# Loading the weights of K and V first: an attention and MLP kernel on one Trainium2 core, with its input DMAs rearranged and one contraction index permuted

## The chip, the cores and the metric

The kernel runs on one core of one Trainium2 chip. The metric is the device time of one execution in microseconds. Before the change it is 720.49 us, the median of three runs (720.48 to 720.58).

The engines are called PE (TensorE, matmul; PEld is its weight load), DVE (VectorE), ACT (ScalarE), POOL (GpSimd) and SP (SyncE, which here only issues DMAs). Each runs its own list of instructions in the order in which they stand, and waits on semaphores for the others. ACT can issue DMAs too; SP and ACT each have a DMA queue of their own.

## The reference

```python
def _A_ref(x, wq, wk, wv, wo):            # x: 1 x 2048 x 512, 32 heads of 16, one K and one V for all heads
    q = (x @ wq).reshape(B, S, H, Dh).transpose(0, 2, 1, 3)
    k = x @ wk
    v = x @ wv
    p = softmax(einsum("bhqd,bkd->bhqk", q, k) * Dh ** -0.5)
    o = einsum("bhqk,bkd->bhqd", p, v)
    return o.transpose(0, 2, 1, 3).reshape(B, S, H * Dh) @ wo

def _B_ref(x, w1, b1, w2, b2):            # w1: 512 x 1792
    return gelu(x @ w1 + b1) @ w2 + b2

xn = layernorm(x)
return x + _A_ref(xn, wq, wk, wv, wo) + _B_ref(xn, w1, b1, w2, b2)
```

All inputs are bf16.

## The kernel before

The kernel has two parts. The first 26 us are a front part that loads the inputs, normalizes x, transposes it, and makes K, V and the first queries. Behind it stands a long loop of scores (PE, line 1086), exponentials (ACT at line 1110, DVE at 1141 with POOL at 1161) and the product with V (PE, line 1154), into which the remaining queries, the MLP and the output projections are woven.

**x and its tiles.** x is 2048 rows of 512 features. It stands in `x_sb` as 16 tiles of 128 rows, a row on a partition. It is loaded in eight pieces, x0 to x7, of two tiles and 256 KB each. The string `X_Q` says for each piece whether SP ("s") or ACT ("a") issues it.

**Layernorm.** For most tiles DVE makes the statistics (`bn_stats`, line 858, then `bn_aggr`, 872); for two tiles ACT does with two passes (855, 865). ACT turns the variance into 1/sigma (877, 879), POOL makes the negated mean `nm` (876, 861) and `nmr` (881). The normalized tile `xn`, which lies in the buffer `ub`, is written by POOL, DVE (both line 895) or ACT (891), as the string `XN_ENG` says.

**Transposes.** PE transposes each tile in four blocks of 128 x 128 (line 914) into PSUM, with the tile as the stationary operand and an identity as the moving one; DVE or ACT (921, 919) copies the result to `xnT`. In `xnT[p, d, s]`, partition p of block d holds one feature of row s. All products that follow contract over this feature: K with `wkp` (line 743, moving 128x512 or 128x256), V and K of single rows with `wvk` (line 743, moving 128x32), the first queries with `wqp` (743), all others with `wq_sb` and the MLP with `w1_sb`. So each of these weights must hold the same feature on the same partition p of the same block d.

**Weights of K and V.** `wvk` holds the 16 columns of wv and of wk for each of the four blocks. POOL copies the wk half into `wkp`, four times side by side (line 810).

**Dummy matmuls.** In the front part the planner also puts matmuls of zeros into PE's order (line 1522, `pro_filler`), where it expects PE to be idle. They are fixed in the order like all others.

**What sets the order.** Every step is recorded with its reads and writes, an estimated duration `occ` and an estimated delay `lat` until others see its result. `Prog.schedule` then plays the program through with these estimates and writes each engine's instructions down in the order that comes out, with the tables (`PRO_DUE` for the front part, `DTAB` and others for the loop) as priorities. On the chip the order is fixed. DMAs are steps of the engine that issues them; `due` and `lat` of a DMA are thus only numbers of this planner.

The places that the prediction speaks of: DVE's first three `bn_stats` wait for x0, x2 and x1, in this order; POOL's line 810 waits for the DMA of wk; PE's dummies at 1522 follow the transposes at 914.

Of the kernel before, what the change touches and what calls it, by code (L numbers as in the profile page):

```python
# [10 lines left out]
P = 128  # L11
# [87 lines left out]
HA = 58  # L99
HB = 168  # L100
LNEXP_SET = 6
X_Q = "sassssss"
X_LAT = (3.1, 3.3, 3.5, 3.6, 3.7, 3.8, 3.8, 3.8)
LAND = (3.8, 4.7, 5.6, 6.4, 7.2, 8.0, 8.7, 9.4)
XN_ENG = "pdpppapadpddddpp"
LN_B = (((0,), "d"), ((1,), "a"), ((2,), "d"), ((3,), "d"), ((4,), "a"), ((5, 8), "d"), ((6,), "d"), ((7,), "d"), ((9,), "d"), ((10,), "d"), ((11,), "d"), ((12,), "d"), ((13,), "d"), ((14,), "d"), ((15,), "d"))
# [23 lines left out]
class Prog:  # L130
# [19 lines left out]
    def add(self, eng, fn, r=(), w=(), acc=None, dma=None, occ=0.1, lat=0.15, allow=1.0, kind=None, tag=None, after=(), due=None, lock=False, docc=0.0, accs=(), chain=None, job=None):  # L150
        op = _Op()
        op.job = job
        op.lock, op.docc = lock, docc
        op.eng, op.fn = eng, fn
        op.stream = dma or eng
        op.amt = 16 if dma else 1
        op.need = bool(dma)
        op.ticket = None
        op.occ, op.lat, op.allow, op.kind, op.tag = occ, lat, allow, kind, tag
        op.idx = len(self.ops)  # L160
        op.done = False
        op.due = due
        op.rel = None
        op.pm = any(k == ("bank", 7) or k[0] == ("bank", 7) for k in (*w, *accs, chain or ("",)))
        deps, sdeps = {}, {}

        def dep(o, raw):
            if o is None or o is op:
                return
            if o.stream == eng == "pe":  # L170
                sdeps.setdefault(id(o), (o, False))
                return
            deps[id(o)] = o
            sdeps[id(o)] = (o, True)

        for k in r:
            dep(self.writer.get(k), True)
            for o in self.accs.get(k, ()):
                dep(o, True)
        for k in w:  # L180
            dep(self.writer.get(k), False)
            for o in self.readers.get(k, ()):
                dep(o, False)
            for o in self.accs.get(k, ()):
                dep(o, False)
        for k in (*((acc,) if acc is not None else ()), *accs, *((chain,) if chain else ())):
            dep(self.writer.get(k), False)
            for o in self.readers.get(k, ()):
                dep(o, False)
        if chain:  # L190
            self.writer[chain] = op
        op.deps = list(deps.values())
        for o in op.deps:
            o.need = True
        for k in w:
            self.writer[k] = op
            self.readers[k] = []
            self.accs[k] = []
        for k in r:
            self.readers.setdefault(k, []).append(op)  # L200
        for k in (*((acc,) if acc is not None else ()), *accs):
            self.accs.setdefault(k, []).append(op)
        for o in after:
            sdeps.setdefault(id(o), (o, kind != "gelu"))
        if self.in_chain:
            o = self.chain.get(eng)
            if o is not None:
                sdeps.setdefault(id(o), (o, False))
            self.chain[eng] = op
        op.sdeps = list(sdeps.values())  # L210
        self.ops.append(op)
        return op
# [401 lines left out]
def bass_parallel_sum__grouped_kv_mqa__dense_activation_gelu__prompt_kernel(  # L614
# [15 lines left out]
    S, D = xf.shape  # L630
    F = B_w1.shape[1]
    assert (S, D, F) == (2048, 512, 1792)
    H, Dh = 32, 16
    NT = S // P
    DT = D // P
# [9 lines left out]
    bf, f32 = dt.bfloat16, dt.float32  # L645
    i16, i32 = dt.int16, dt.int32

    with ExitStack() as es:
        def sb(shape, dtype, name):
            return es.enter_context(nc.sbuf_tensor(name, shape, dtype))  # L650
# [3 lines left out]
        ubs = (ub, x_sb)  # L654
        xn = ub[:, 0:8, :]
        xnT = sb([P, DT, S], bf, "xnT")
        wvk = sb([P, DT, 2 * Dh], bf, "wvk")
        oTp = sb([P, NPR, TBW], bf, "oTp")
        wkp = oTp[:, 1, :].rearrange("p (d a n) -> p d a n", d=DT, a=4)
        wq_sb = sb([P, DT, D], bf, "wq_sb")  # L660
# [5 lines left out]
        w1_sb = sb([P, DT, F], bf, "w1_sb")  # L666
        w2_sb = sb([P, FT, D], bf, "w2_sb")
        b1row = sb([P, P], bf, "b1row")
        b1T = sb([P, FT], f32, "b1T")
        ident = sb([P, P], bf, "ident")  # L670
# [47 lines left out]
        def bank(b, n=1):  # L718
            return pAll[:, b * 512:(b + n) * 512]
# [4 lines left out]
        add = pr.add  # L724

        def B(b):
            return ("bank", b)
# [9 lines left out]
        def mm(o, l, rh, start, stop, r=(), w=(), tp=None, skip=False, occ=0.216, allow=1.5, **ak):  # L737
            kw = {}
            if tp is not None:
                kw["tile_position"] = tp  # L740
            if skip:
                kw["skip_group_check"] = True
            return add("pe", lambda e: e.matmul(o, l, rh, start=start, stop=stop, **kw), r, w, occ=occ, lat=dlat[1],  # L743
                       allow=allow, **ak)
# [26 lines left out]
        def dma(eng, o, i, stream, r=(), w=(), lat=2.2, allow=1.0, **kw):  # L771
            return add(eng, lambda e: e.dma_start(o, i), r, w, dma=stream, occ=0.7, lat=lat, allow=allow, **kw)

        x_view = xf.rearrange("(t p) d -> p t d", p=P)
        for i in range(8):
            e = X_Q[i]
            dma("sp" if e == "s" else "act", x_sb[:, 2 * i:2 * i + 2, :], x_view[:, 2 * i:2 * i + 2, :], f"d_x{i}",
                w=[("x", 2 * i), ("x", 2 * i + 1)], lat=X_LAT[i], due=0.0)
        dma("sp", wvk[:, :, Dh:2 * Dh], A_wk.rearrange("(k p) n -> p k n", p=P), "d_wk", w=["wk_s"], due=0.1, lat=3.0)
        dma("sp", wvk[:, :, 0:Dh], A_wv.rearrange("(k p) n -> p k n", p=P), "d_wv", w=["wv_s"], due=0.2, lat=3.0)  # L780
        dma("sp", wq_sb[:], A_wq.rearrange("(k p) n -> p k n", p=P), "d_wq", w=["wq"], due=0.4, lat=8.0)
        dma("sp", w1_sb[:], B_w1.rearrange("(k p) n -> p k n", p=P), "d_w1", w=["w1"], due=0.5, lat=9.0)
        dma("sp", w2_sb[:], B_w2.rearrange("(k p) n -> p k n", p=P), "d_w2", w=["w2"], due=0.7, lat=15.0)

        def setup(fn, r=(), w=(), occ=0.16, due=0.0, lat=0.1, **kw):
            return add("pool", fn, r, w, occ=occ, lat=lat, due=due, **kw)
# [19 lines left out]
        for g0, g1, f, kw in ((0, Q0_SPLIT, dve, dict(n=Q0_SPLIT * TBW // 2)), (Q0_SPLIT, NGR, setup, dict(occ=0.24 * (NGR - Q0_SPLIT)))):  # L806
            if g0 < g1:
                f(lambda e, g0=g0, g1=g1: e.memset(QT[:, g0:g1, :].rearrange("p g n -> p (g n)").bitcast(f32), 0.0),
                  w=[(k, g, j) for k in ("QT", "QTm") for g in range(g0, g1) for j in range(HG)], **kw)
        setup(lambda e: e.tensor_copy(wkp[:, :, :, 0:Dh], wvk[:, :, Dh:2 * Dh].unsqueeze(2).to_broadcast([P, DT, 4, Dh])),  # L810
              r=["wk_s", "wkp"], w=["wkp"], occ=0.35, due=2.0)

        setup(lambda e: e.tensor_copy(ident_f[:], ident[:]), r=["ident"], w=["ident_f"])
# [20 lines left out]
        def act_set():  # L834
# [4 lines left out]
                    n=1500, due=0.01)  # L839
# [62 lines left out]
        def x_T(ts, bk, eng):  # L902
            n = len(ts)
            for ti in ts:
                normed(ti)
            c = slice(ts[0] * P, (ts[-1] + 1) * P)
            parts = ((0, 2, bk, "a"), (2, 4, (bk + 1) % 3, "d")) if eng == "s" else ((0, DT, bk, eng),)
            for d0, d1, bk, eng in parts:
                m = (d1 - d0) * n
                pT = bank(bk)[:, 0:m * 64].bitcast(bf)  # L910
                for k, ti in enumerate(ts):
                    for d in range(d0, d1):
                        o = ((d - d0) * n + k) * P
                        add("pe", lambda e, ti=ti, d=d, o=o, pT=pT: e.transpose(pT[:, o:o + P], xn[:, ti % 8, d * P:(d + 1) * P], ident[:]),  # L914
                            r=[("u", 0, ti % 8), "ident"], w=[B(bk)], occ=0.069)
                src, dst = pT.rearrange("p (k n) -> p k n", k=d1 - d0), xnT[:, d0:d1, c]
                w = [B(bk)] + [("xnT", ti, h) for ti in ts for h in range(d0 // 2, d1 // 2)]
                if eng == "a":
                    act(lambda e, src=src, dst=dst: e.activation(dst, src, ACT.Copy), w=w, n=m * P)
                else:  # L920
                    dve(lambda e, src=src, dst=dst: e.tensor_copy(dst, src), w=w, n=m * P, mode=2)
# [12 lines left out]
        def vbank(a, b):  # L934
            return (pO[:, a * 32:b * 32], "O") if a < NVA else (bank(5)[:, (a - NVA) * 32:(b - NVA) * 32], B(5))
# [42 lines left out]
        def v_tiles(ts):  # L978
            for ti in ts:
                for d in range(DT):  # L980
                    mm(vbank(ti, ti + 1)[0], xnT[:, d, ti * P:(ti + 1) * P], wvk[:, d, :], d == 0, d == DT - 1,
                       r=["wv_s", "wk_s", ("xnT", ti, d // 2)], w=[vbank(ti, ti + 1)[1]], occ=0.036, kind="v")

        def wq_first():
# [8 lines left out]
        for _, _, kind, a in sorted(steps, key=lambda s: s[:2]):  # L993
# [15 lines left out]
            due=0.0)  # L1009
# [8 lines left out]
        for va, vb_ in ((0, NVA), (NVA, NT)):  # L1018
# [3 lines left out]
                n=(vb_ - va) * Dh, mode=2)  # L1022
# [445 lines left out]
        first, n = None, 0  # L1468
        for t in range(NTILE):
            if is_d[t]:  # L1470
                first, n = (t, 1) if n == 0 else (first, n + 1)
# [41 lines left out]
        for g in range(4):  # L1513
            mm4(pM, oT[:, g * P:(g + 1) * P], wol[:, g, :], False, g == 3, r=[("oTl", g // 2)] + WOL,
                w=[B(7)], due=0.0)
# [48 lines left out]
```

## Time and the profile before

| | |
|---|---|
| median of 3 runs | 720.49 us |
| the profiled execution's own time | 722.47 us |
| its span, first to last instruction | 720.6 us |
| first exponential of the loop (ACT, line 1110) | at 26.25 us |
| PE, DVE, ACT, POOL busy | 98%, 97%, 98%, 63% of the span |
| DMA in the first fortieth of the span (18 us) | 280 GB/s |
| DMA over the whole span | 33 GB/s |

In a timeline or a chain a row begins with the start in us from the span's start and the duration in us; then come engine, line, operation and what it writes and reads. A bracket at the end tells how long the engine was idle before and what ended that. A busy PE is not PE at its peak, since matmuls overlap: the distance between their starts tells the pace.

### The profile page before, as it was taken

What the parts mean: (1) busy time and instruction counts of PE and PEld (TensorE: products, weight loads), DVE (VectorE), ACT (ScalarE), POOL (GpSimd) and SP (SyncE); (2) the same over time, 40 slices, a digit from 0 to 9 for tenths busy, and PEclk for the clock granted to TensorE, in tenths of its full rate; (3) what the DMA queues carried; (4) which work ended last, traced back from release to release, by engine and by line L of the source; (5) the groups of instructions that cost most, each with busy time, mean ns of one, the idle gap of its engine ahead of it and who ended that gap; (6) DMA issues with size and microseconds to landing.
All of it is one profiled execution on the core that took longest, in us unless ns stands there. A gap on an engine that the chain in (4) does not pass through costs nothing.

```text
span 720.6 us, 22619 instructions
## 1 busy us (share of the span) xinstructions
PE 706.1 (98%) x9224; PEld 219.9 (31%) x9224; DVE 699.6 (97%) x1387; ACT 703.9 (98%) x762; POOL 451.0 (63%) x739
## 2 busy tenths in 40 slices
PE   7999999999999999999999999999999999999998
PEld 4332232222243332223222232222233222222233
DVE  7899999999998999999999999999999999999986
ACT  6899999999999999999999999999999999999997
POOL 7455556777633446687777645676775786766531
PEclk9999999999999999999999999999999999999999
DMA  8300100101011010010101110110100110111111
GB/s 280 108 10 17 26 16 10 33 13 29 10 35 30 24 33 18 12 30 19 37 11 26 46 39 19 25 19 16 24 17 17 26 32 18 32 24 33 26 31 40
DMA packets 36254, 23.59 MB, mean 33 GB/s; under 512 B 17768, under 2 KB 32568, under 8 KB 36152
## 3 DMA queue, kind: packets, MB, share of 16 engines
q1 hardware_dynamic: 35880, 21.89, 12.1%
q8 instruction: 74, 1.21, 0.7%
q10 hardware_dynamic: 272, 0.26, 0.1%
q14 instruction: 28, 0.23, 0.1%
HBM read 13.28 MB, written 2.35 MB: 22 GB/s over the span
## 4 chain that ended last, share of the span: by engine, by line
ACT 52%; PE 42%; DVE 3%; POOL 1%; issue 1%; DMA 0%; POOLq 0%
ACT E L1110 49%; PE pAll L1154 21%; PE pAll L1086 13%; PE pAll L767 6%; PE pAll L749 2%; DVE Dt L1141 2%; ACT ub L1343 1%; ACT x_sb L1348 1%; PE pAll L743 1%; DVE Dt L1194 1%; DMA x_sb<-in_A_x_dram 0%; DVE Dt L1162 0%; PE pAll L914 0%; POOL ub L895 0%; ACT x_sb L1343 0%
## 5 line engine op out<-in xcount | busy, mean ns | idle before, releaser
L1110 ACT ACTIVATE E<-pAll 128x1024 bf16<-128x1024 f32 (+2 forms) x676 | 652.2, 1146 | 2.9 <-PE pAll L1086 1.2
L1161 POOL INT64_ADD Dt<-Dt x671 | 429.0, 648 | 246.8 <-DVE Dt L1141 80.1
L1141 DVE TENSOR_SCALAR Dt<-pAll 128x512 int16<-128x512 f32 (+1 forms) x599 | 414.3, 710 | 6.5 <-PE pAll L763 4.4
L1154 PE MATMUL pAll<-Dt,V 128*32 128x512 bf16 x3120 | 417.1, 383 | 0.0
L1154 PE MATMUL pAll<-E,V 128*32 128x512 bf16 x1424 | 284.5, 385 | 0.5 <-DVE Of L1240 0.4
L1086 PE MATMUL pAll<-QT,KT 32*128 32x512 bf16 x2048 | 266.6, 384 | 5.5 <-ACT E L1110 4.2
L1194 DVE TENSOR_SCALAR Dt<-Dt 128x1024 int16<-128x1024 int16 (+7 forms) x291 | 162.0, 567 | 2.2 <-PE pAll L1154 1.9
L1086 PEld LDWEIGHTS pAll<-QT,KT 32*128 32x128 bf16 x2048 | 66.5, 90 | 276.5 <-ACT E L1110 260.8
L1154 PEld LDWEIGHTS pAll<-Dt,V 128*32 128x32 bf16 x3120 | 106.8, 94 | 115.4 <-issue 79.5
L1162 DVE TENSOR_SCALAR Dt<-Dt 128x1024 int16<-128x1024 int16 (+1 forms) x270 | 90.9, 366 | 0.1
L1154 PEld LDWEIGHTS pAll<-E,V 128*32 128x32 bf16 x1424 | 65.7, 94 | 49.1 <-issue 38.5
L767 PE MATMUL pAll<-xnT,w_sb 128*32 128x512 bf16 x520 | 70.5, 382 | 0.0
L767 PE MATMUL pAll<-w_sb,ub 128*32 128x512 bf16 x364 | 49.4, 381 | 0.0
L763 PE MATMUL pAll<-w_sb,x_sb 32*128 32x512 bf16 x116 | 44.6, 384 | 0.1
L767 PE MATMUL pAll<-w_sb,x_sb 128*32 128x512 bf16 x276 | 42.1, 382 | 0.0
L763 PE MATMUL pAll<-xnT,w_sb 32*128 32x512 bf16 x88 | 33.8, 384 | 0.0
L763 PE MATMUL pAll<-w_sb,ub 32*128 32x512 bf16 x84 | 32.3, 384 | 0.0
L767 PE MATMUL pAll<-wop,oTp 128*32 128x512 bf16 x192 | 29.4, 382 | 0.0
L767 PEld LDWEIGHTS pAll<-xnT,w_sb 128*32 128x32 bf16 x520 | 18.3, 95 | 10.9 <-issue 5.2
L763 PE MATMUL pAll<-xnT,wq_sb 32*128 32x512 bf16 x56 | 21.5, 384 | 0.0
L1320 DVE TENSOR_SCALAR ub<-pAll,b1T 128x512 bf16<-128x512 f32 x28 | 20.9, 747 | 0.0
L767 PE MATMUL pAll<-xnT,wq_sb 128*32 128x512 bf16 x200 | 20.7, 383 | 0.2
(135 smaller groups left out, 361.8 us busy)
## 6 DMA issues: line engine op xcount, KB each, us to landing
w_sb<-in_B_w_dram SPq DMA_DIRECT2D x2, 1792.0 KB, 12.4
OfP<-Of SPq DMA_DIRECT2D x96, 32.0 KB, 2.0
rbP<-rden_rows SPq DMA_DIRECT2D x96, 32.0 KB, 1.9
x_sb<-in_A_x_dram SPq DMA_DIRECT2D x16, 128.0 KB, 2.2
QT<-qp SPq DMA_DIRECT2D x124, 16.0 KB, 1.8
out_dram<-x_sb SPq DMA_DIRECT2D x15, 128.0 KB, 1.7
x_sb<-in_A_x_dram SPq DMA_DIRECT2D x7, 256.0 KB, 5.4
OfP<-Of SPq DMA_DIRECT2D x56, 16.0 KB, 1.9
```

The source lines that it names most:

```text
L743: return add("pe", lambda e: e.matmul(o, l, rh, start=start, stop=stop, **kw), r, w, occ=occ, lat=dlat[1], allow=allow, **ak)
L749: add("pe", lambda e, c=c, j=j: e.matmul(o[c, :], l[:, c], rh, start=start, stop=stop, tile_position=(0, 32 * j)), r, [(k, j) for k in w] ...
L763: add("pe", lambda e, b, c=c, j=j: e.matmul(pM, l[c, :], rh[c, :], start=False, stop=b, skip_group_check=True, tile_position=(32 * j, 0)), ...
L767: add("pe", lambda e, b, c=c, j=j: e.matmul(pM[c, :], l[:, c], rh, start=n == 0, stop=b, skip_group_check=True, tile_position=(0, 32 * j)) ...
L1086: ins = e.matmul(o, l, rh, start=True, stop=True, tile_position=(q0, 0))
L1110: o = act(lambda e: e.activation(E[:, s0:s0 + na, :], bank(b0, na).rearrange("p (a n) -> p a n", a=na), ACT.Exp, scale=LN2 / 128.0), w=[B( ...
L1141: op = dve(lambda e: e.tensor_scalar(Dt[:, s:s + n, :], bank(bk, n).rearrange("p (a n) -> p a n", a=n), float(127 * 128) + SPL_D, SPL_MIN, ...
L1154: add("pe", lambda e, a, b: e.matmul(pO[32 * j:32 * j + 32, :], V1[:, v, kt, :], rhs, start=a, stop=b, tile_position=(0, 32 * j)), r=r + [ ...
L1161: return e.int64_add(d.bitcast(dt.uint64), x.bitcast(dt.uint64), k * 0x0001000100010001 % 2 ** 64)
L1162: return e.tensor_scalar(d, x, float(k), None, ALU.add)
L1194: dve(lambda e, d=view(o, nb), q=view(i, nb), k=k: e.tensor_scalar(d, q, float(k), None, ALU.add), r=keys(i), w=keys(o), n=nb * n * TBW, m ...
L1320: dve(lambda e: e.tensor_scalar(ubs[tb % 2][:, ft, :], pM, b1T[:, ft:ft + 1], None, ALU.add), r=["b1T"], w=M4 + [ukey(tb, ft)], n=TBW + 57 ...
```

## The change

It has three parts.

1. The two DMAs of wk and wv move from SP's queue, behind the seven pieces of x there, to the front of ACT's queue. The piece x1, which ACT issued, becomes the second of eight on SP's queue.
2. The weights wk, wv, wq and w1 are loaded with `(p k) n` in place of `(k p) n`: partition p holds the features 4p, 4p+1, 4p+2 and 4p+3 in its four blocks, in place of p, 128+p, 256+p and 384+p. So a partition reads one unbroken stretch: 128 bytes of wk or wv in place of four of 32, 4 KB of wq in place of four of 1 KB, 14 KB of w1 in place of four of 3.5 KB. `wvk` becomes `[P, 2, DT, Dh]`, with wv and wk in halves of their own.
3. So that `xnT` holds the same features, the transposes take every fourth feature of a row (`d:D:DT`) in place of 128 neighbours. `w2` and `wo` contract over something else and stay.

The planner's `due` and `lat` of the DMAs are set so that its order of everything else comes out as it was; PE's, DVE's and POOL's instructions stand in the same order.

```diff
-X_Q = "sassssss"
-X_LAT = (3.1, 3.3, 3.5, 3.6, 3.7, 3.8, 3.8, 3.8)
+X_Q = "ssssssss"
+X_LAT = (3.1, 3.9, 2.8, 2.9, 3.0, 3.1, 3.1, 3.1)
...
-        wvk = sb([P, DT, 2 * Dh], bf, "wvk")
+        wvk = sb([P, 2, DT, Dh], bf, "wvk")
...
-        dma("sp", wvk[:, :, Dh:2 * Dh], A_wk.rearrange("(k p) n -> p k n", p=P), "d_wk", w=["wk_s"], due=0.1, lat=3.0)
-        dma("sp", wvk[:, :, 0:Dh], A_wv.rearrange("(k p) n -> p k n", p=P), "d_wv", w=["wv_s"], due=0.2, lat=3.0)
-        dma("sp", wq_sb[:], A_wq.rearrange("(k p) n -> p k n", p=P), "d_wq", w=["wq"], due=0.4, lat=8.0)
-        dma("sp", w1_sb[:], B_w1.rearrange("(k p) n -> p k n", p=P), "d_w1", w=["w1"], due=0.5, lat=9.0)
+        dma("act", wvk[:, 1], A_wk.rearrange("(p k) n -> p k n", k=DT), "d_wk", w=["wk_s"], due=-0.1, lat=6.6)
+        dma("act", wvk[:, 0], A_wv.rearrange("(p k) n -> p k n", k=DT), "d_wv", w=["wv_s"], due=0.0, lat=6.6)
+        dma("sp", wq_sb[:], A_wq.rearrange("(p k) n -> p k n", k=DT), "d_wq", w=["wq"], due=0.4, lat=8.7)
+        dma("sp", w1_sb[:], B_w1.rearrange("(p k) n -> p k n", k=DT), "d_w1", w=["w1"], due=0.5, lat=9.7)
...
-        setup(lambda e: e.tensor_copy(wkp[:, :, :, 0:Dh], wvk[:, :, Dh:2 * Dh].unsqueeze(2).to_broadcast([P, DT, 4, Dh])),
+        setup(lambda e: e.tensor_copy(wkp[:, :, :, 0:Dh], wvk[:, 1].unsqueeze(2).to_broadcast([P, DT, 4, Dh])),
...
-                        add("pe", lambda e, ti=ti, d=d, o=o, pT=pT: e.transpose(pT[:, o:o + P], xn[:, ti % 8, d * P:(d + 1) * P], ident[:]),
+                        add("pe", lambda e, ti=ti, d=d, o=o, pT=pT: e.transpose(pT[:, o:o + P], xn[:, ti % 8, d:D:DT], ident[:]),
...
-                    mm(vbank(ti, ti + 1)[0], xnT[:, d, ti * P:(ti + 1) * P], wvk[:, d, :], d == 0, d == DT - 1,
+                    mm(vbank(ti, ti + 1)[0], xnT[:, d, ti * P:(ti + 1) * P], wvk[:, :, d, :], d == 0, d == DT - 1,
```

ACT's order at its beginning, with - before and + now (`wvk` is the tile of the weights of V and K; the last two rows are the first steps of layernorm on ACT):

```order
 L611 UNCONDITIONAL_BRANCH
 L838 ACT_TABLE_LOAD
-L772 DMA x_sb<-in_A_x_dram 128x2x512
+L772 DMA wvk<-in_A_wk_dram 128x64
+L772 DMA wvk<-in_A_wv_dram 128x64
 L855 ACTIVATE oTp,sm<-x_sb 128x512
 L877 ACTIVATE lnv<-mv,epsc 128x1
```

ACT now issues wk and wv where it issued x1, ahead of its first arithmetic.

SP's order at its beginning (`w_sb` stands for w1 and then w2):

```order
 L611 UNCONDITIONAL_BRANCH
-L772 DMA x_sb<-in_A_x_dram 128x2x512 x7
-L772 DMA wvk<-in_A_wk_dram 128x4x16
-L772 DMA wvk<-in_A_wv_dram 128x4x16
-L772 DMA wq_sb<-in_A_wq_dram 128x4x512
-L772 DMA w_sb<-in_B_w_dram 128x4x1792
+L772 DMA x_sb<-in_A_x_dram 128x2x512 x8
+L772 DMA wq_sb<-in_A_wq_dram 128x2048
+L772 DMA w_sb<-in_B_w_dram 128x7168
 L772 DMA w_sb<-in_B_w_dram 128x14x512
 L772 DMA wop<-in_A_wo_dram 128x4x512
```

SP issues one more piece of x and no longer wk and wv; wq and w1 follow one DMA earlier.

More of the change, by code (lines that the diff above doesn't have):

```diff
@@ L778, in bass_parallel_sum__grouped_kv_mqa__dense_activation_gelu__prompt_kernel @@
                 w=[("x", 2 * i), ("x", 2 * i + 1)], lat=X_LAT[i], due=0.0)
-        dma("sp", wvk[:, :, Dh:2 * Dh], A_wk.rearrange("(k p) n -> p k n", p=P), "d_wk", w=["wk_s"], due=0.1, lat=3.0)
-        dma("sp", wvk[:, :, 0:Dh], A_wv.rearrange("(k p) n -> p k n", p=P), "d_wv", w=["wv_s"], due=0.2, lat=3.0)
-        dma("sp", wq_sb[:], A_wq.rearrange("(k p) n -> p k n", p=P), "d_wq", w=["wq"], due=0.4, lat=8.0)
-        dma("sp", w1_sb[:], B_w1.rearrange("(k p) n -> p k n", p=P), "d_w1", w=["w1"], due=0.5, lat=9.0)
-        dma("sp", w2_sb[:], B_w2.rearrange("(k p) n -> p k n", p=P), "d_w2", w=["w2"], due=0.7, lat=15.0)
+        dma("act", wvk[:, 1], A_wk.rearrange("(p k) n -> p k n", k=DT), "d_wk", w=["wk_s"], due=-0.1, lat=6.6)
+        dma("act", wvk[:, 0], A_wv.rearrange("(p k) n -> p k n", k=DT), "d_wv", w=["wv_s"], due=0.0, lat=6.6)
+        dma("sp", wq_sb[:], A_wq.rearrange("(p k) n -> p k n", k=DT), "d_wq", w=["wq"], due=0.4, lat=8.7)
+        dma("sp", w1_sb[:], B_w1.rearrange("(p k) n -> p k n", k=DT), "d_w1", w=["w1"], due=0.5, lat=9.7)
+        dma("sp", w2_sb[:], B_w2.rearrange("(k p) n -> p k n", p=P), "d_w2", w=["w2"], due=0.7, lat=15.7)
         def setup(fn, r=(), w=(), occ=0.16, due=0.0, lat=0.1, **kw):
```

## The prediction

> **What bounds the kernel now.** I read the page first.
>
> ```profile
> span 720.6 us, 22619 instructions
> PE 706.1 (98%) x9224; PEld 219.9 (31%) x9224; DVE 699.6 (97%) x1387; ACT 703.9 (98%) x762; POOL 451.0 (63%) x739
> ```
>
> Three engines are busy for 97 to 98% of the span. The exp loop, which starts at 26 us, has next to no slack, and the change touches none of its instructions. What can move is the moment at which the loop starts. So I read the chain of work for the first 40 us (start, us, what).
>
> ```profile
> 0.80 3.51 DMA x_sb<-in_A_x_dram
> ...
> 9.33 1.38 issue
> ...
> 10.73 0.40 POOL oTp L810
> ...
> 11.60 0.77 POOL ub L895
> 12.41 0.61 PE pAll L914 x4
> ...
> 26.25 7.44 ACT E L1110 x8
> ```
>
> The chain runs through POOL, whose instructions stand in a fixed order. From 9.33 to 10.71 POOL does nothing. The view of waits for this stretch names the cause, and the DMA issues of single stretches tell when each piece lands (after the size: us from issue to landing). The rows are x1 (the ACT one), then on SP's queue x2, x7, wk and wv. The timeline has their issues; the seven x issues on SP take 0.47 of 3.53 us each and follow every 0.51 us from 0.80.
>
> ```profile
> POOL oTp L810 <- DMA wvk<-in_A_wk_dram: 1.4, 1, 1.4
> x_sb<-in_A_x_dram ACTq DMA_DIRECT2D x1, 256.0 KB, 3.8
> x_sb<-in_A_x_dram SPq DMA_DIRECT2D x1, 256.0 KB, 4.0
> x_sb<-in_A_x_dram SPq DMA_DIRECT2D x1, 256.0 KB, 6.6
> wvk<-in_A_wk_dram SPq DMA_DIRECT2D x1, 16.0 KB, 6.3
> wvk<-in_A_wv_dram SPq DMA_DIRECT2D x1, 16.0 KB, 6.0
> 0.80 3.53 SPq L772 DMA_DIRECT2D x_sb<-in_A_x_dram  x7
> 4.37 0.47 SPq L772 DMA_DIRECT2D wvk<-in_A_wk_dram  x1
> 4.88 0.54 SPq L772 DMA_DIRECT2D wvk<-in_A_wv_dram  x1
> ```
>
> So wk lands at 4.37 + 6.3 = 10.7 us, because it stands behind x7, which lands at 3.87 + 6.6 = 10.5. POOL reaches its copy L810 at 9.33 and waits until then. Behind L810 on POOL stand the rows of `nm`, `nmr` and the normalization L895, and PE waits for that.
>
> **The change part by part.**
>
> *The wait on wk goes.* wk is issued first on ACT's queue, at about 0.82. On that queue 256 KB took 3.8 us, so 16 KB is there by 4.6, far ahead of 9.33. POOL gains 1.38 us, and its L895 that ended at 12.37 ends at 10.99. What is late next? The timeline of PE and DVE:
>
> ```profile
> 5.38 1.29 DVE L858 BATCH_NORM_STATS2 stats<-x_sb 128x6 f32<-128x512 bf16 x2
> 8.57 0.70 DVE L895 TENSOR_SCALAR ub<-x_sb,nm,rstd 128x512 bf16<-128x512 bf16 x1
> 9.32 1.03 PE L914 MATMUL pAll<-ident,ub 128*128 128x128 bf16 x8 [0.29 <-DVE ub L895]
> 10.15 1.49 PE L1522 MATMUL pAll<-zeros 128*128 128x256 bf16 x6
> 12.41 0.61 PE L914 MATMUL pAll<-ident,ub 128*128 128x128 bf16 x4 [0.78 <-POOL ub L895]
> ```
>
> PE has transposes (L914) and six dummy matmuls (L1522) ahead of the transposes that wait for POOL. The dummies end at 10.15 + 1.49 = 11.64, and they are in PE's order whether needed or not. So of POOL's 1.38 us only PE's idle time of 0.78, from 11.64 to 12.41, can be gained: **-0.77 us**. PE's own chain is late next: the dummies follow L914 at 9.32, that follows DVE's L895 at 8.57, and that DVE has worked without a break since 5.38, when its second `bn_stats` had waited for x2 (1.31 + 4.0 = 5.3).
>
> *The pieces of x.* Whatever delays x2 takes as much from the gain. Before, x2 was on SP behind x0 while x1 came on the other queue; now x0 and x1 stand ahead of it on one queue, so the same bytes are ahead, plus wk and wv. Price of wk and wv: on SP they landed about 0.2 us each after their predecessor (10.5, 10.7, 10.9) with 512 pieces of 32 bytes; with 128 of 128 bytes I take a quarter to the whole, 0.1 to 0.4 for both. Price of one queue instead of two, from the windows (last column GB/s):
>
> ```profile
> 4.00:4.50 0.50, 0.50 (x4) 0.32 (x3) 0.17 (x1) 0.17 (x1) 0.49 (x3) 1.00 1.09 383
> 4.50:5.00 0.50, 0.50 (x4) 0.15 (x1) 0.50 (x1) 0.50 (x2) 0.40 (x3) 1.00 1.08 342
> 6.00:7.00 1.00, 0.00 (x0) 0.00 (x0) 1.00 (x4) 1.00 (x5) 0.84 (x7) 1.00 1.06 350
> ```
>
> Two queues moved 383 and one 342 to 350: over the 1.5 us in which x1 and x2 arrive that is at most 0.15. x0 alone at the front may land up to 0.3 sooner, which frees nothing, since x2 sets DVE's start. I take **+0.2** (0 to +0.5). x1 itself may come 0.5 later than its 0.82 + 3.8 = 4.6; DVE reads it in the second of the two `bn_stats` of the 5.38 row, at about 6.0, so that is free.
>
> *PE's pace.* The groups of PE from 9 to 16.6 us, then from 16.9 to 25 (mean ns of one behind the bar):
>
> ```profile
> L914 PE MATMUL pAll<-ident,ub 128*128 128x128 bf16 x22 | 3.1, 310 | 1.1 <-POOL ub L895 0.8 <-DVE ub L895 0.3
> L914 PE MATMUL pAll<-ident,ub 128*128 128x128 bf16 x37 | 3.9, 220 | 0.1
> 16.77 0.35 PEld L743 LDWEIGHTS pAll<-wvk,xnT 128*128 128x128 bf16 x10
> 18.38 0.17 PEld L914 LDWEIGHTS pAll<-ident,ub 128*128 128x128 bf16 x3 [0.22 <-ACT ub L891]
> ```
>
> The same transpose takes 310 ns early and 220 late; eight from 9.32 step by 0.104, so PE runs at half pace until about 16.7. If that moment stays, the 0.57 us of work that moves ahead of it costs up to 0.28 more, and PE's idle 0.22 before 18.38 takes part of that: 0.06 to 0.28, I take **+0.15**.
>
> *The transposes read every fourth element.* The stationary operand of all 64 is now strided. A contiguous load of 128 columns steps by (0.35 - 0.10) / 9 = 0.028 us (L743, above), a transpose by 0.104 slow and about 0.055 fast. The load hides behind the matmul ahead of it until it is two to four times as long. I take 0; the other end is a rival below. [...]
>
> *Edits at nothing.* V's matmuls read 2 runs of 16 instead of 32, as many elements. The copy L810 reads the same 64 elements a partition. wq and w1 go in fewer, larger packets and are issued about 0.5 sooner; their readers are far off.
>
> ```profile
> L985 POOL COPY oTp<-wq_sb x1: 396/396/396, 16.8 to 16.8; 128x256 bf16<-128x256 bf16 x1
> wq_sb<-in_A_wq_dram SPq DMA_DIRECT2D x1, 512.0 KB, 6.5
> w_sb<-in_B_w_dram SPq DMA_DIRECT2D x2, 1792.0 KB, 12.4
> L767 PEld LDWEIGHTS pAll<-xnT,w_sb x520: 92/95/97, 41.9 to 533.8; 128*32 128x32 bf16 x174
> ```
>
> wq, issued at 5.46, lands at 12.0 and is read at 16.8; w1 is read first at 41.9.
>
> Sum: -0.77 + 0.2 + 0.15 = **-0.42 us** at the start of the loop. Everything behind 26.25 stands in a fixed order on engines that are full, so the end moves by as much: a span of 720.2 for 720.6. The profiled execution's own time was 722.47, 1.98 above the median of 720.49 (its recording is in it); I take the difference over to the median: 720.07, so 720.1. A measurement of this kernel can tell about 0.2%, 1.44 us, from no change.
>
> **The rivals.**
>
> *PE reaches its full pace earlier (faster).* PE was unbroken for 3.81 us at the front (the 17 dummies, row below) and stayed slow; it was unbroken from 12.41 and was fast 4.3 us later.
>
> ```profile
> 1.33 3.81 PE L1522 MATMUL pAll<-zeros 128*128 128x256 bf16 x17 [1.33 <-POOL mask L825]
> 15.16 1.06 PE L743 MATMUL pAll<-xnT,oTp 128*128 128x512 bf16 x2
> ```
>
> With the idle 0.78 gone, PE works unbroken from about 9.5, so 4.3 us of it are reached at 13.8. Then the work that would stand from 13.8 to 16.2, 2.4 us, could take half, 1.2 less; copies on ACT and DVE between it (about 1 us each) do not shrink, so I take 0.75 of it and drop the term for the pace: -0.57 - 0.75 = -1.3, 719.2 (718.6 to 719.7). [...] 28%.
>
> *Strided weight loads show (slower).* Place: L914. It decides from the point where a load takes longer than the transpose it hides behind, 0.055 to 0.104 us. Four times 0.028 is 0.11: nothing in the slow part, +0.055 for each of the 37 transposes of the later group, +2.0. Eight times is 0.22: +0.12 x 22 + 0.17 x 37 = +8.9 at most. I take the lower: -0.4 + 2.0 = 722.1 and up (721.5 to 729). Nothing in the trace reads a strided stationary operand. 13%.
>
> *The x pieces come later than I take it.* If x2 slips by 0.8 or more, PE's chain is as late as POOL was and the gain is gone: 720.5, and for a slip of 1.0 with x4 and x6, which DVE also meets just landed, 720.8 (720.5 to 721.2). For it: DVE has nothing else to do at 5.38. Against: the same bytes, and wk and wv are 32 KB beside 768. 10%.
>
> *The wait does not go* (wk lands after 9.33 even so): it would need 8.5 us for 16 KB at the front of a queue that gave 256 KB in 3.8. Below 1%, and left out.
>
> **How the numbers follow.** The forecast has 49%, its own range 719.6 to 720.5. Faster by over 0.2% means below 719.05: half of the early-pace case, 0.14. Slower by over 0.2% means above 721.93: nearly all of the strided case and a little of the late x, 0.13. The rest is 0.73. The range from 718.8 to 721.2 holds the forecast, the late x and nearly all of the early pace; it leaves out the strided case and the early pace's lower end, together under 2 in 10.
>
> **What would show it.** Right: no idle time before L810; L810 at about 9.3 to 9.5 on POOL; PE's row L914 x4 at 11.8 to 12.0 with no idle time ahead of it; DVE's second L858 at 5.4 to 5.8; the first E row at 25.7 to 26.0. The early pace would show as 128x512 matmuls of L743 (1.06 us for two at 15.16 before) at the fast duration before 16 us. Strided loads would show as L914 steps above 0.055 late or longer PEld rows. I am wrong if the loop starts where I say and the end moves otherwise, or if x2 lands before 5.3.

## The result and the profile after

The changed kernel is 721.56 us in the median (720.97 to 722.44, 20 runs), before 720.56 (720.14 to 721.86, 20 runs): ratio 1.0014 [1.0007, 1.002]. It is slower by 1.0 us; it was forecast 0.4 us faster. Two later comparisons on other chips gave 1.0005 [0.9996, 1.0014] and 1.0008 [0.9999, 1.0016], medians 0.65 and 0.30 above before. So the loss is 0.3 to 1.0 us by the medians, within the 0.2% that count as no change; only the first of the three intervals excludes 1.

The first profiled execution of the changed kernel took 722.15 us. Its page begins:

```profile
span 720.3 us, 22619 instructions
PE 704.5 (98%) x9224; PEld 219.5 (30%) x9224; DVE 698.8 (97%) x1387; ACT 704.0 (98%) x762; POOL 451.5 (63%) x739
```

The instruction count is that of before, and span and busy times nearly so. The first 26 us look different. POOL's timeline there:

```profile
9.25 0.21 POOL L876 TENSOR_SCALAR nm<-mv 128x1 f32<-128x1 f32 x1 [1.70 <-DVE mv L872]
...
10.78 0.39 POOL L810 COPY oTp<-wvk 128x256 bf16<-128x256 bf16 x1
11.14 0.22 POOL L876 TENSOR_SCALAR nm<-mv 128x2 f32<-128x2 f32 x1
```

L810 no longer waits for wk, yet it starts at 10.78, where it had stood at 10.73 before. POOL's wait has moved upstream: 1.70 us at 9.25, for DVE's `mv`. DVE and PE show why:

```profile
7.14 1.29 DVE L858 BATCH_NORM_STATS2 stats<-x_sb 128x6 f32<-128x512 bf16 x2 [2.45 <-DMA x_sb<-in_A_x_dram]
...
10.82 1.04 PE L914 MATMUL pAll<-ident,ub 128*128 128x128 bf16 x8 [2.58 <-DVE ub L895]
11.66 1.49 PE L1522 MATMUL pAll<-zeros 128*128 128x256 bf16 x6
12.94 0.63 PE L914 MATMUL pAll<-ident,ub 128*128 128x128 bf16 x4
```

DVE's second `bn_stats` waited 2.45 us for x2 and began at 7.14 instead of 5.38. The chain of work to the loop now runs through exactly these rows (start, us, what):

```profile
1.81 5.30 DMA x_sb<-in_A_x_dram
7.14 1.29 DVE stats L858 x2
...
10.82 1.04 PE pAll L914 x8
11.87 1.28 PE pAll L1522 x6
13.15 0.43 PE pAll L914 x4
...
25.97 7.44 ACT E L1110 x8
```

x2 was issued at 1.81 and took 5.30 us. The loop begins at 25.97; its distance to the end of the span is 694.3 us, as in before (720.6 - 26.25 = 694.35). In all but one of the profiles of this study this distance is 694.3 to 694.4 (the exception is in the last section). So all that the change does is done by the first E row.

Seen alone, these two profiles seem to bear the forecast out: the loop begins at 25.97 instead of 26.25, and the span is 720.3 instead of 720.6. That is luck. The profiled execution of before lay 1.98 us above its kernel's median, that of the changed kernel 0.59.

### The profile page after: what moved, and what is told of

It is laid out like the page before. It is cut to its first block, busy times and chain, and to the rows that moved or that the text cites. A ratio compares the mean times of both kernels' runs of the same rounds, so it can differ in the third digit from the quotient of the medians.

```text
span 720.3 us, 22619 instructions
## 1 busy us (share of the span) xinstructions
PE 704.5 (98%) x9224; PEld 219.5 (30%) x9224; DVE 698.8 (97%) x1387; ACT 704.0 (98%) x762; POOL 451.5 (63%) x739
## 4 chain that ended last, share of the span: by engine, by line
ACT 52%; PE 43%; DVE 4%; DMA 1%; issue 0%; SPq 0%
ACT E L1110 49%; PE pAll L1154 21%; PE pAll L1086 13%; PE pAll L767 6%; PE pAll L749 2%; DVE Dt L1141 2%; ACT ub L1343 1%; DMA x_sb<-in_A_x_dram 1%; ACT x_sb L1348 1%; PE pAll L914 1%; DVE Dt L1194 1%; PE pAll L743 0%; DVE Dt L1162 0%; DVE stats L858 0%; ACT x_sb L1343 0%
## 5 line engine op out<-in xcount | busy, mean ns | idle before, releaser
L1194 DVE TENSOR_SCALAR Dt<-Dt 128x1024 int16<-128x1024 int16 (+7 forms) x291 | 160.2, 560 | 2.2 <-PE pAll L1154 1.9
L1162 DVE TENSOR_SCALAR Dt<-Dt 128x1024 int16<-128x1024 int16 (+1 forms) x270 | 89.4, 357 | 0.1
```

What stands on the lines that cost most here:

```text
L1162: return e.tensor_scalar(d, x, float(k), None, ALU.add)
L1194: dve(lambda e, d=view(o, nb), q=view(i, nb), k=k: e.tensor_scalar(d, q, float(k), None, ALU.add), r=keys(i), w=keys(o), n=nb * n * TBW, m ...
```

## The experiments

The theory after the result was D: with x1 moved from ACT's queue to SP's, x2 lands later, and DVE, then PE, wait for it. Its rivals were that the loads of wk and wv beside x are to blame, that the strided transposes cost, or that only the executions or the chips differ; each expectation says which theory it speaks of. Each comparison with before is within one chip. In the table "x2 row" is the start of DVE's second L858 in the profiled execution and "loop" the first E row. The ratio is worked out from the same runs, but it is not the quotient of the two medians: the last two columns can differ by up to 0.4 us. Where an edit moves a DMA, the planner's `lat` numbers move with it, so that the order of everything else stays; the diffs below leave these lines out.

| kernel | x2 row | loop | span | median minus before | ratio |
|---|---|---|---|---|---|
| before2 | 5.54 | 24.31 | 718.7 | one run | |
| rows_only | 5.79 | 25.57 | 719.9 | -0.10 | 0.9994 [0.9985, 1.0003] |
| x_one_queue | 6.38 | 25.32 | 719.7 | +1.41 | 1.0014 [1.0005, 1.0022] |
| x_one_queue2 | 6.54 | 25.98 | 720.3 | +1.22 | 1.0015 [1.0007, 1.0024] |
| x1_on_act | 4.55, x1 7.95 | 26.80 | 721.2 | +1.62 | 1.0019 [1.001, 1.0029] |
| after2 | 6.07 | 24.73 | 719.1 | one run | |
| after3 | 5.55 | 24.85 | 720.5 | +0.65 | 1.0005 [0.9996, 1.0014] |
| after4 | 5.93 | 24.59 | 718.9 | +0.30 | 1.0008 [0.9999, 1.0016] |
| after_old_rows | 5.92 | 25.38 | 719.7 | +0.04 | 1.0001 [0.9992, 1.001] |
| after_old_rows2 | 5.83 | 25.10 | 719.5 | +0.55 | 1.0004 [0.9995, 1.0013] |
| kv_behind_x1 | 5.74 | 25.15 | 719.5 | -0.13 | 0.9997 [0.9988, 1.0005] |
| kv_behind_x1b | 5.74 | 24.57 | 718.9 | -0.17 | 0.9993 [0.9985, 1.0002] |
| x1x3_on_act | 5.73 | 24.38 | 718.7 | -0.23 | 0.9998 [0.9989, 1.0007] |
| x2_behind_x3 | 6.14 | 25.37 | 719.7 | +0.43 | 1.0003 [0.9994, 1.0012] |
| x2_on_act | 5.50 | 24.10 | 718.5 | -0.64 | 0.9993 [0.9984, 1.0002] |
| after_no6 | 5.85 | 25.42 | 719.7 | +1.45 | 1.0019 [1.001, 1.0029] |

**before2** is before once more.

> The kernel before once more, for a second profile of it. The changed kernel's profile has x2 landing at 7.12 us where before had 5.35. Theory A (x2's lateness belongs to the change): here x2 lands at 5.2 to 5.6 us again and wk at 10.5 to 11. Theory B (landings differ that much from execution to execution of one kernel): x2 lands somewhere between 5.3 and 7.2. The moment at which PE's pace rises (16.7 us before, 15.3 after) is expected to differ here by up to some us under both.

It took 720.50 us; the other runs of before on this chip have a median of 720.91. x2 came as theory A has it (row at 5.54), wk earlier than it has it (10.0). The rows on POOL and PE:

```profile
10.04 0.40 POOL L810 COPY oTp<-wvk 128x256 bf16<-128x256 bf16 x1 [0.60 <-DMA wvk<-in_A_wk_dram]
...
10.26 1.38 PE L1522 MATMUL pAll<-zeros 128*128 128x256 bf16 x6
11.72 0.40 PE L914 MATMUL pAll<-ident,ub 128*128 128x128 bf16 x4
```

The wait for wk is 0.60 here instead of 1.38, and PE's four transposes follow the dummies, which end at 11.64, after 0.08 us. wk's DMA row shows where the 0.7 us went (last column: us from issue to landing). It was issued at 4.37 in both, and in the first profile it had taken 6.3:

```profile
wvk<-in_A_wk_dram SPq DMA_DIRECT2D x1, 16.0 KB, 5.6
```

So in this execution the wait that the change removes was hidden behind PE's dummies nearly whole. The first profile, at 722.47, was an execution on the long side. Two kernels below with wk at its old place behind x7, rows_only and x2_behind_x3, agree with the second: POOL goes on to L810 without a wait (at 9.67 and 9.78).

**rows_only** is before with `(p k) n` and the strided transposes, queues as before.

```diff
-A_wk.rearrange("(k p) n -> p k n", p=P)           # wk, wv, wq, w1
+A_wk.rearrange("(p k) n -> p k n", k=DT)
-e.transpose(pT[:, o:o + P], xn[:, ti % 8, d * P:(d + 1) * P], ident[:])
+e.transpose(pT[:, o:o + P], xn[:, ti % 8, d:D:DT], ident[:])
```

> The kernel before with nothing changed but the layout: wk, wv, wq, w1 in whole rows, feature 4p+k on partition p, transposes of every fourth feature; queues as before. Theories Q and S: x2 at 5.3 to 5.6 us, wk some 0.3 us sooner than 10.7, time 0 to 0.4 us below before. Theory R: 0.8 us or more above before, with steps of the transposes over 0.055 us where PE is fast.

-0.10 us, an interval that holds 1. Seven strided transposes at full pace, and seven contiguous ones of before2:

```profile
16.34 0.56 PE L914 MATMUL pAll<-ident,ub 128*128 128x128 bf16 x7
```

```profile
15.04 0.55 PE L914 MATMUL pAll<-ident,ub 128*128 128x128 bf16 x7
```

The strided stationary operand costs nothing that shows. x2's row, at 5.79, is a little later than the 5.3 to 5.6 of Q and S.

**x_one_queue** is before with x1 on SP's queue, behind x0; wk, wv and the later weights keep their places behind the last x, one issue later.

```diff
-X_Q = "sassssss"
+X_Q = "ssssssss"
```

> The kernel before with nothing changed but x1, which is second of eight pieces on SP's queue; wk and wv behind x7 on SP with their old rows. Theory Q: x2 lands at 6.5 to 7.2 us and the time is 0.6 to 1.2 us above before. Theory S: x2 lands at 5.3 to 5.7 us and the time is within 0.3 us of before.

+1.41 us, and the interval excludes 1: this one move gives the loss, a little above theory Q's 1.2. DVE waits for x2:

```profile
6.38 1.29 DVE L858 BATCH_NORM_STATS2 stats<-x_sb 128x6 f32<-128x512 bf16 x2 [1.80 <-DMA x_sb<-in_A_x_dram]
```

But x2 is not what comes last here. wk too is issued 0.5 us later, and the chain of this profile runs through it (start, us, what):

```profile
4.88 5.91 DMA wvk<-in_A_wk_dram
...
10.84 0.10 POOL oTp L810
...
11.70 0.77 POOL ub L895
...
12.52 0.62 PE pAll L914 x4
```

On the way of x2, PE's eight transposes begin at 10.06 (first row), in before2 at 9.43 (second row):

```profile
10.06 1.04 PE L914 MATMUL pAll<-ident,ub 128*128 128x128 bf16 x8 [1.31 <-DVE ub L895]
```

```profile
9.43 1.04 PE L914 MATMUL pAll<-ident,ub 128*128 128x128 bf16 x8 [0.34 <-DVE ub L895]
```

That is 0.63 us later; the four at the chain's end begin 0.80 us later (12.52 against 11.72). So x2 accounts for most of the shift in this profile and wk for the rest. In the changed kernel wk is early, and only the first part is left.

The windows show that the transfers thin out just when x0 and x1 have arrived (last columns: DMA share, GB/s). First before2, then x_one_queue on the same chip, then the changed kernel's first profile:

```profile
4.00:4.50 0.50, 0.50 (x4) 0.33 (x3) 0.06 (x1) 0.06 (x1) 0.49 (x3) 1.00 1.09 385
4.50:5.00 0.50, 0.43 (x4) 0.13 (x1) 0.50 (x1) 0.50 (x2) 0.40 (x3) 1.00 1.08 379
```

```profile
4.00:4.50 0.50, 0.50 (x4) 0.33 (x3) 0.47 (x2) 0.39 (x2) 0.49 (x3) 1.00 0.96 262
4.50:5.00 0.50, 0.50 (x4) 0.15 (x1) 0.08 (x1) 0.07 (x1) 0.50 (x4) 1.00 0.91 227
```

```profile
4.00:4.50 0.50, 0.50 (x4) 0.32 (x3) 0.48 (x1) 0.50 (x2) 0.49 (x3) 1.00 1.12 236
4.50:5.00 0.50, 0.50 (x4) 0.15 (x1) 0.18 (x1) 0.07 (x2) 0.50 (x4) 1.00 0.90 229
```

In before2, with a big piece at the head of both queues, 379 to 385 GB/s run on; in the other two, with one queue of big pieces, it falls to 227 to 262. In the later profiles of the changed kernel (after2, after3, after4) these windows have 254 to 338, so the dip is not always as deep. In the six rows above the DMA share stays at 0.90 to 1.12, so by this measure the DMA engines are not idle meanwhile. What the one queue lacks at that moment the trace does not show.

**x1_on_act** is the changed kernel with x1 back on ACT's queue, but behind wk and wv.

```diff
-X_Q = "ssssssss"
+X_Q = "sassssss"          # order on ACT: wk, wv, x1
```

> The changed kernel with x1 back on ACT's queue, behind wk and wv; whole rows and everything else as changed. Theory Q (x1 on SP's queue ahead of x2 is what makes x2 late): x2 lands at 5.3 to 5.6 us, POOL does not wait for wk, time 0.3 to 0.8 us below before, 720.56 -> about 720.0. Theory S (the small packets of wk and wv at the front are what make x2 late): x2 lands at 6.5 to 7.2 us, time 0.5 to 1.2 us above before. Theory R (the strided transposes cost it): 0.8 us or more above before with x2 at 5.3 to 5.6.

+1.62 us, so this does not cure the loss. x2 came early, but x1 took 6.1 us from its issue, and DVE waited for that one:

```profile
4.55 0.69 DVE L858 BATCH_NORM_STATS2 stats<-x_sb 128x6 f32<-128x512 bf16 x1
7.95 0.69 DVE L858 BATCH_NORM_STATS2 stats<-x_sb 128x6 f32<-128x512 bf16 x1 [2.70 <-DMA x_sb<-in_A_x_dram]
```

Again the third big piece is the late one, whichever it is. None of the three theories had this. To have two queues isn't enough: with wk and wv at the head of ACT's the loss is there too.

**after2**, **after_old_rows**, **kv_behind_x1** and **x1x3_on_act** shared a chip. after_old_rows has the changed queues with the old layout. In kv_behind_x1 x1 stays at the head of ACT's queue and wk and wv, in whole rows, follow it there; x1x3_on_act has x1, x3, wk, wv there.

```diff
-X_Q = "ssssssss"          # order on ACT: wk, wv
+X_Q = "sassssss"          # kv_behind_x1, order on ACT: x1, wk, wv
```

> The changed kernel once more, for a second profile. [...] Theory L (the 7.12 of the first profile was one execution's luck): x2 at 5.4 to 6.0.

> The changed kernel with the old rows: wk and wv first on ACT's queue as 512 pieces of 32 bytes each, all of x on SP's queue, transposes of neighbouring features. [...] Theory R (strided transposes are the cost): time back at or below before.

> Pieces of x as before (x1 first on ACT's queue), wk and wv in whole rows behind x1 on ACT's queue. Theory D: x2 lands at 5.3 to 5.8 us as before, wk by 5.5 us, POOL does not wait for it, and the time is 0.4 to 0.9 us below before. Theory S (small packets of wk and wv among the first transfers stall the engines wherever they stand): x2 at 6 us or later and no gain.

> x1 and x3 on ACT's queue, wk and wv behind them there, the other six pieces on SP's. Theory D: with two queues feeding the engines there is no dip of the DMA rate between 3.75 and 6 us; x2 at 5.0 to 5.6, x4 to x7 by 0.3 us sooner than before; wk by 6.5; time 0.4 to 1.0 us below before. Theory S: the dip is there again, x2 at 6 or later.

The two with x1 at the head of ACT's queue have x2's row at 5.74 and 5.73 and no loss; the two with x1 on SP's queue have it at 6.07 and 5.92. The 6.07 is just past theory L's 5.4 to 6.0 and 1.07 us before the first profile's 7.14; the gains of 0.4 us and more that theory D gave kv_behind_x1 and x1x3_on_act did not come (-0.13 and -0.23). The loss itself hardly showed on this chip (after_old_rows +0.04). That leaves open whether it hangs on the chip, which is rival C of the next expectations.

**after3**, **x_one_queue2** and **after_old_rows2**, on a third chip, repeat the comparison.

> The changed kernel once more, timed on the same chip as the two kernels beside it. Theory D (moving x1 onto SP's queue makes the third piece x2 land 0.5 to 1.8 us later, DVE's statistics wait for it, and PE's whole chain behind them shifts): x2 after 6.0 us, the second DVE L858 after it, PE L914 x4 at 11.9 to 13.0, and the median 0.6 to 1.2 us above before. Rival C (the loss of the first result came from the chip or the executions drawn): within 0.3 us of before.

> Before, with only x1 moved from ScalarE's queue to second place on SP's. Theory D: as the changed kernel, 0.7 to 1.4 us above before, x2 at 6.0 us or later. Rival R (the whole-row loads of wk and wv on the other queue take the place of x's packets and so delay x2): no loss here, since wk and wv stand behind x; x2 at 5.3 to 5.8 us.

> The changed kernel with the old layout of the four weights (wk, wv, wq, w1 in 32-element or 512-element rows, contiguous transposes), queues as changed. Theory D: the queue of x1 alone matters, so it lies within 0.3 us of the changed kernel beside it, and above before by 0.3 us or more. Rival W (the layout of the weight loads matters): it lies near before, as its single earlier comparison had it, while the changed kernel beside it is 0.6 us or more above it.

x_one_queue lost as much as before (+1.22), the changed kernel 0.65 and its old-layout twin 0.55. So the layout makes no difference that shows (against W), and having wk early seems to give back 0.6 of what x1's move costs (721.26 against 721.83). D's lower bound of 0.6 for the changed kernel held by a hair, and the interval holds 1. D's rows were missed in after3's profile: x2's is at 5.55 and the four transposes at 11.41, both sooner than it had them. There the chain runs through x6, a later piece of the one queue. In x_one_queue2 it runs through x3:

```profile
3.86 5.74 DMA x_sb<-in_A_x_dram
...
9.62 1.29 DVE stats L858 x2
```

```profile
2.32 5.88 DMA x_sb<-in_A_x_dram
...
8.21 0.69 DVE stats L858
```

So it is not always x2 that comes last. In after, after2 and after4 it is.

**after_no6** is the changed kernel without the six dummies between L914 x8 and x4.

```diff
-list(self.fill_deps), self.pro_filler, (None, 0)
+list(self.fill_deps), None if 20 <= nfill < 26 else self.pro_filler, (None, 0)
```

> The changed kernel without the six dummy matmuls that stand between the transposes x8 and x4 on PE. By the chain of the changed kernel these six take 1.28 us between the end of the transposes that the late x2 releases and the four that POOL's chain releases, whose input is long there. Theory L (what is late is the chain, and PE's pace is not set by those six): the four transposes start at once behind the eight, the loop starts up to 1.3 us earlier, and the median falls by 0.5 to 1.3 us below the changed kernel. Rival P (the dummies buy PE's full pace): the pace rises one period of 3.4 us later in most executions, and the median is the same as the changed kernel's or up to 0.8 us above it.

722.06 against after3's 721.26: slower by 0.8. The four transposes did not start at once; POOL's chain was late next:

```profile
9.54 1.04 PE L914 MATMUL pAll<-ident,ub 128*128 128x128 bf16 x8 [1.29 <-DVE ub L895]
11.52 0.62 PE L914 MATMUL pAll<-ident,ub 128*128 128x128 bf16 x4 [0.94 <-POOL ub L895]
```

PE idles there for 0.94 us. The windows of this execution and then of after4 (PEclk is the third number from the end) show 26 matmuls at 0.50 where after4 does 37 at 0.85:

```profile
11.50:14.50 3.00, 2.75 (x26) 2.44 (x28) 3.00 (x9) 2.85 (x10) 2.93 (x10) 0.50 0.97 407
```

```profile
11.50:14.50 3.00, 2.72 (x37) 2.24 (x35) 3.00 (x10) 2.70 (x9) 2.84 (x11) 0.85 0.91 382
```

The six dummies are worth more than they cost; the median speaks for rival P. The later rise is seen in one profile of each, so that it is the cause is possible and not shown.

**after4** and **kv_behind_x1b** share a chip with **x2_behind_x3**, which is before with x3 issued ahead of x2 on SP's queue, so that x2 is late for another reason.

```diff
-    w=[("x", 2 * i), ("x", 2 * i + 1)], lat=X_LAT[i], due=0.0)
+    w=[("x", 2 * i), ("x", 2 * i + 1)], lat=X_LAT[i], due=(-0.8, -0.7, -0.5, -0.6, -0.4, -0.3, -0.2, -0.1)[i])
```

> The changed kernel again, beside a kernel that differs from it in x1's queue alone. Theory D: 0.5 to 1.2 us above before; x2 after 5.5 us and later than in the kernel beside it. Rival C (the loss hangs on the chip): within 0.3 us of before here.

> The changed kernel's whole rows and its wk and wv on ScalarE's queue, but x1 stays at the front of that queue as before. Theory D: the loss is x1's move alone, so this one lies 0.5 to 1.3 us below the changed kernel and 0 to 0.3 us below before; x2 at 5.3 to 5.8 us, L810 without a wait. Rival W (any wk and wv beside x at the front cost x its bandwidth): it lies with the changed kernel.

> Before with x3 issued ahead of x2 on SP's queue, x1 on ScalarE's queue as before: x2 lands one step later (6.0 to 6.6 us), with both queues busy at the front, nothing else moved. Theory D (x2's landing itself sets the chain, however it comes late): 0.5 to 1.2 us above before, like x_one_queue, with PE L914 x8 at 9.9 to 10.6. Rival Q (one queue at the front costs in another way than through x2, or the chain has room for a later x2): within 0.3 us of before.

The changed kernel was at 721.21, kv_behind_x1b at 720.74 (-0.47; its highest run, 721.04, is below 7 of the 11 of after4). In both wk is early; what differs is x1's queue, and with it whether wk and wv head ACT's. Their two profiles do not show the loss: x2's rows differ by 0.19 us and the loops begin at 24.59 and 24.57. x2_behind_x3 was 0.43 above before, with nothing moved but x2 and x3, which changed places:

```profile
6.14 1.29 DVE L858 BATCH_NORM_STATS2 stats<-x_sb 128x6 f32<-128x512 bf16 x2 [0.92 <-DMA x_sb<-in_A_x_dram]
...
9.82 1.03 PE L914 MATMUL pAll<-ident,ub 128*128 128x128 bf16 x8 [1.35 <-DVE ub L895]
```

That is D's direction, but under D's lower bound of 0.5, as after4's 0.30 is under its own, and the interval holds 1. By itself it would be weak; it agrees with the rest. Rival C is not excluded as to the size: with x1 on SP's queue and wk early the loss was 1.0, about 0, 0.6 and 0.3 us in the four comparisons.

**x2_on_act** is kv_behind_x1b with x1 and x2 exchanged: x2 at the head of ACT's queue, x1 second on SP's, as the change has it.

```diff
-X_Q = "sassssss"
+X_Q = "ssasssss"          # order on ACT: x2, wk, wv
```

> As kv_behind_x1b, but x2 and not x1 stands at the front of ScalarE's queue, and x1 is second on SP's. Both queues still begin with a big piece. Theory D (x2's landing sets DVE's second L858 and the chain; a big piece at the front of each queue keeps the front full): x2 at 4.3 to 4.8 us, x1 at 5.3 to 5.8, DVE goes on without a wait behind the first tile at about 5.2, PE L914 x8 at 8.8 to 9.1, and the median 0.1 to 0.6 us below before, at or below kv_behind_x1b. Rival S (x1 second on SP's queue is what hurts, whatever stands on ScalarE's): x1 after 6.0 us, DVE waits for it, and the median is 0.4 us or more above before.

720.68 against 721.32 of before on that chip, ratio 0.9993 [0.9984, 1.0002]. DVE no longer waits behind the first tile, though x0 itself came late in this profile, at 4.65:

```profile
4.67 0.70 DVE L858 BATCH_NORM_STATS2 stats<-x_sb 128x6 f32<-128x512 bf16 x1 [1.86 <-DMA x_sb<-in_A_x_dram]
...
5.50 1.25 DVE L858 BATCH_NORM_STATS2 stats<-x_sb 128x6 f32<-128x512 bf16 x2
```

x2 landed at 5.0 and x1 at 6.0, and PE's next transposes began at 9.22, all a little later than expected. So x1's place as second on SP does no harm while a big piece heads the other queue (against S). With kv_behind_x1 and x1x3_on_act this is the best of the versions; all four comparisons came out 0.1 to 0.6 us below before, and none of the intervals excludes that there is no gain. All four lie below the changed kernel's 0.3 to 1.0 above before.

## Why the prediction was wrong

*The term of -0.77, the wait on wk.* The wait went, as said. But the term was at least 0.5 us too big, since it was sized from one execution in which the last pieces of x landed late. In before2 the wait is 0.60 and all of it but 0.08 lies behind the six dummies: kv_behind_x1b, where wk is early and x2 at 5.74, has PE's four transposes at 11.47, before2 at 11.72 (shown above).

```profile
11.47 0.39 PE L914 MATMUL pAll<-ident,ub 128*128 128x128 bf16 x4
```

There is 0.25 us to be had at most, and the medians show 0.1 to 0.2, not clear of nothing. The working put the 1.98 us between that execution and the median down to its recording; before2, also profiled, took 720.50, so it was the execution.

*The term of +0.2 for x2, bound 0.5.* This is the step that failed. The working said "the same bytes are ahead" and priced one queue by steady windows at 0.15. x2's row came 0.2 to 1.8 us later than 5.38 (5.55, 5.93, 6.07, 7.14 in four profiles), over the bound in three of four, and 0.84 later in x_one_queue than in before2. The steady windows (342 to 350 GB/s) do not hold for the first pieces: the rate fell to 227 to 262 when the second piece was in. x2's issue moved from 1.31 to 1.81, by 0.5 us. In the two profiles with only x1 moved its row is later than before2's by more than that, 0.84 and 1.00; the changed kernel's four, 0.01 to 1.60 after it, lie on both sides. So whether one queue costs x2 more than the shift of its issue is not settled by the runs.

*The sum.* With at most -0.25 for wk and 0.2 to 1.8 for x2 in place of -0.77 and +0.2, and the +0.15 for PE's pace as it stood, the sum is a loss of 0.1 us or more.

*The rival of the late x* was the right one. It stood at 10% and gave 720.5 for a slip of 0.8, as a gain of 0.77 given back, and 720.8 for 1.0; its range ended at 721.2, under the 721.56 measured. The slip was 0.2 to 1.8, and there was next to no gain to set against it. The prediction's own "what is late next" named the chain that the changed kernel then showed: x2, L858, L895, L914 x8, the dummies, L914 x4.

*PE's pace.* Neither the fixed moment of 16.7 nor the rival of 4.3 us unbroken work holds. The moment is one thing in one execution and another in the next of the same kernel. kv_behind_x1b and kv_behind_x1 have x2's row at 5.74 both; in the windows they differ:

```profile
11.50:14.50 3.00, 2.70 (x39) 1.93 (x39) 3.00 (x10) 3.00 (x11) 2.92 (x12) 1.00 0.94 387
```

```profile
11.50:14.50 3.00, 3.00 (x29) 2.49 (x28) 2.86 (x9) 2.70 (x8) 2.84 (x11) 0.50 0.95 388
```

The first has 39 matmuls at full pace from 11.5 to 14.5, the second 29 at half, and their loops begin at 24.57 and 25.15. The other profiles sort the same way. Where PEclk stays at 0.50 for 3.41 us after its fall, the loop begins at 24.10 to 24.85 (seven profiles); where it stays for 6.83 us, at 25.10 to 25.98 (eight). Three profiles (before, x_one_queue, x1_on_act) can't be sorted so: PEclk is 1.00 throughout the front, though their eight transposes at 9 to 11 us take 1.03 to 1.05 us, against 0.62 and 0.64 for eight behind the rise in before2 and kv_behind_x1b.

This goes a good way to explain how 0.4 us of a late x2 can become up to 1 us in the median: work that comes later may more often be caught by the second stretch at half pace. The profiles with two stretches have a mean granted clock of 0.995, those with one 0.997 or 0.998 (after3, with its second fall, apart). 25 of 42 executions of the changed kernel had 0.995 or less, 46 of 130 of before, and 10 of 56 of the five kernels with a big piece at the head of both queues and whole rows. In before those executions have a median of 721.51, the others 720.63. The others include executions at 0.999 or 1.000, which by the three profiles above need not have run faster, so the counts are rough. That the late x2 causes the shift in these shares is an inference from the counts; no run set the phase of the pace. Nor does a run separate the late x2 from the gap that it leaves: with x1 behind it x0 lands sooner (first L858 at 3.69 to 3.79 in the changed kernel, 4.33 and 4.45 in before), so PE stands idle for 1.05 to 2.58 us ahead of its eight transposes, in before for 0.29 and 0.34.

*The strided loads* cost nothing that shows (rows_only: -0.10 us, seven transposes in 0.56 us against 0.55; the 0 was the author's estimate), and *the edits at nothing* were nothing. The loop's start carried over to the span one to one (694.3 to 694.4 us from the first E row to the end, with one exception).

## What to carry to other kernels

At this kernel's start it was best to put a big transfer that the first compute step needs at the head of each DMA queue, and the small ones behind it (0.1 to 0.6 us below before in four comparisons): here the small early transfers cost the big one behind them more than they gained (x1_on_act, +1.62 us, against kv_behind_x1, -0.13). Before pricing a wait, look at it in a second execution; a wait that lies behind work fixed in another engine's order may already be free in the usual one, as all but 0.08 of the 0.60 us was in before2. And name what is late next before counting a gain, then price its own inputs as carefully as the wait that goes.

## What the runs showed of the hardware

PE was at half pace for 3.41 us in kv_behind_x1b (7.96 to 11.38 us) and for 6.83, twice as long, in kv_behind_x1 (8.26 to 15.09). The moments shift from execution to execution (rises at 11.2 to about 13 us in some profiles, 14.4 to 16.8 in others). In after3 the pace fell once more as the loop began, and it is the one profile whose loop takes longer (720.5 - 24.85 = 695.65 us, 1.3 more):

```profile
24.90:25.90 1.00, 0.36 (x3) 0.06 (x3) 1.00 (x4) 1.00 (x2) 0.92 (x2) 1.00 0.00 0
26.10:29.30 3.20, 3.20 (x25) 0.54 (x22) 1.72 (x3) 2.40 (x3) 1.04 (x3) 0.50 0.03 6
```

PE is busy for all 3.2 us there at PEclk 0.50, while ACT is busy for only 2.40.
